# A fused attention and expert kernel: gates in a ring of five, one block sum formed later and in place, scratch shared

## The chip, the cores and the metric

The kernel runs on one core of one Trainium2 chip. Times are device microseconds of one execution. The engines are TensorE (PE, with PEld for its weight loads), VectorE (DVE), ScalarE (ACT), GpSimd (POOL) and the Sync engine (SP), from whose queue the stores of the output and the loads of the gates are issued.

A ratio of two kernels is the mean time of one kernel's runs over that of the other's of the same rounds, with a 95% interval, so it is not quite the ratio of the medians that stand beside it.

## The reference, cut to what matters

```python
def reference(**kwargs):            # cut: q, k, v are [4, 8, 768, 64]
    # attention: 4 sink keys, and a causal window of 128 keys
    attn_out = _attn_ref(**attn_kwargs)
    x = attn_out.transpose(0, 2, 1, 3).reshape(3072, 512)
    # four experts, every token through all of them
    p = domain_probs / (domain_probs.sum(-1, keepdims=True) + 1e-09)
    out = 0
    for e in range(4):
        h = np.maximum(x @ w1[e], 0.0)          # [3072, 1024]
        out += p[:, e:e + 1] * (h @ w2[e])      # [3072, 512]
    return out
```

## The kernel before

Tokens are handled in pairs of two 128-row tiles: three pairs a batch element, twelve pairs. The first batch element is done directly. For the other nine pairs, the second product (H times w2) is done with seven block products instead of eight (the scheme of Strassen and Winograd), P1 to P7. It needs sums of blocks of H on VectorE, in which H11 and H12 are the two halves of the first row tile and H21 and H22 those of the second. For each pair and each expert:

```python
# first product: 4 groups (j) of 8 matmuls per expert, each group evicted by VectorE
nc.vector.scalar_tensor_tensor(out=dst, in0=h, scalar=0.0, in1=gate, op0=ALU.max, op1=ALU.mult)
...
# sums(): as soon as an H block (all four groups of an expert) is there
nc.vector.tensor_add(S[0][:, e], H21, H22)          # operand of P5
nc.vector.tensor_sub(H21, H11, H21)                 # operand of P7, in place
nc.vector.tensor_sub(S[1][:, e], S[0][:, e], H11)   # operand of P6
...
for u in list(self.last):                           # operand of P3
    b, g, e = u
    if busy((b, g), "P3") or t["dve"] < self.stored:
        break
    ...
    nc.vector.tensor_sub(S[2][:, e], self.H[b, g, e][:, 1, :, 0], S[1][:, e])
...
CHAIN = ("P1", "P2", "P6", "P5", "P7", "P4", "P3")  # order of the products of a pair
```

The program is laid out by a scheduler inside the kernel's Python, which keeps its own estimate of each engine's time and picks the next piece of TensorE work. In a late pair it alternates products with single groups of H for the next pair (P1, group, P2, group, ..., P3), and then issues the ten remaining groups of that next pair without a product between. I call that the **dense stretch**. There are six H buffers. H groups go through four PSUM banks, which VectorE must empty.

The softmax here doesn't subtract the row's maximum and nothing guards it: scores larger than these inputs give would overflow.

Of the kernel before, what the change touches and what calls it, by code (L numbers as in the profile page):

```python
# [16 lines left out]
def kernel(  # L17
# [12 lines left out]
    nc = tc.nc  # L30
# [29 lines left out]
    TURN = 3500  # L60
# [6 lines left out]
    bank_free = {tag: [0.0] * n for tag, n in (("mix", 1), ("r", 4))}  # L67
# [24 lines left out]
    def free_at(tag, n=1):  # L92

        return max(bank_free[tag][:n])

    def take(tag, until):
        bank_free[tag].pop(0)
        bank_free[tag].append(until)
# [157 lines left out]
    dp = mo.tile([NT, P, E], FP32, name="dp", tag="osb", bufs=1)  # L256
# [4 lines left out]
    def gates_by_row():  # L261
        ds = mo.tile([NT, P], FP32, name="ds", tag="ds", bufs=1)
        pn = mo.tile([NT, E, P], FP32, name="pn", tag="hr", bufs=1)
        nc.vector.reduce_sum(out=ds, in_=dp, axis=AX.X)
        nc.vector.tensor_scalar_add(out=ds, in0=ds, scalar1=1e-9)
        nc.vector.reciprocal(out=ds, in_=ds)
        nc.vector.tensor_mul(
            pn, dp.rearrange("n p e -> n e p"), ds[:, None, :].to_broadcast([NT, E, P]),
        )
        for i in range(2):  # L270
            nc.sync.dma_start(out=gate_rows[:, :, i, :], in_=pn[i:NT:2])
        dve(1800, 0.0)
# [3 lines left out]
    def load_gates(pair):  # L276

        x = mo.tile([P, E, 2, P], FP32, name="gates", tag="gates", bufs=2)
        nc.sync.dma_start(
            out=x.rearrange("p e t n -> p (e t n)"),  # L280
            in_=gate_rows[pair].rearrange("e t n -> (e t n)").partition_broadcast(P),
        )
        gate_sb[pair] = x
        sp()
# [3 lines left out]
    zeros = mo.tile([P, 2 * G], BF16, name="zeros", tag="hr", bufs=1)  # L288
# [9 lines left out]
    identf = consts.tile([P, P], FP32, name="identf")  # L298
# [76 lines left out]
    def two_banks(tag="mix"):  # L375

        if tag == "mix":
            x = psum.tile([P, 2, 2 * G], FP32, name="sps", tag="mix", bufs=1)
            return [x[:, 0], x[:, 1]], x
        return [psum.tile([P, 2 * G], FP32, name="sps", tag=tag, bufs=4) for _ in range(2)], None  # L380

    def transposes(b, g, hp, tag="mix"):

        if b not in qkT:
            qkT[b] = sb.tile([P, 2, NHP, S], BF16, name="qkT", tag="qkT", bufs=1)
        if (b, g, hp) == (0, 0, 0):
            cast_first(0)
        tr = psum.tile([P, 2, 2, P], BF16, name="tr", tag=tag, bufs=1 if tag == "mix" else 4)
        hs = slice(2 * hp, 2 * hp + 2)
        for i in range(2):  # L390
            for tt in range(2):
                rows = first["qk"[i]][:, tt, hs] if (b, g) == (0, 0) else nat[b, 2 * g + tt][:, i, hs]
                nc.tensor.transpose(tr[:, i, tt], rows, ident)  # L393
        done = pe(4 * P, cast_at[hp // 2] if (b, g) == (0, 0) else rows_at(b, g), free_at(tag), n=4)
        dst = qkT[b][:, :, hp, g * G:(g + 1) * G]
        if (b, g) == (0, 0):
            for i, engine in enumerate(("dve", "act")):
                copy(engine, dst[:, i].rearrange("c (p t) -> c p t", t=2), tr[:, i].rearrange("c t p -> c p t"))
            at = max(act(2 * P, done), dve(2 * P, done))
        else:  # L400
            engine, at = sooner(4 * P, done)
            copy(engine, dst, tr.rearrange("c i t p -> c i (t p)"))
        take(tag, at)
        turned_at[b, g, hp] = at
        if (b, g, hp) == (0, 0, 1):
            cast_first(1)
        if hp == NHP - 1:
            for _ in range(2):
                qkn_free.remove(1e12)
                qkn_free.append(done)  # L410
            qkn_free.sort()
# [11 lines left out]
    def sink_values(b):  # L423
        vsd[b] = sb.tile([P, NHP, 2, DX], BF16, name="vsd", tag="vsd", bufs=2)
# [11 lines left out]
    def sinks(b, piece):  # L436
# [4 lines left out]
        sp, _ = two_banks()  # L441
# [14 lines left out]
    def scores(b, hp, g, tag="mix"):  # L456
        T = qkT[b]
        w = sum(x[2] for x in GROUPS[g]) * P
        sps, both = two_banks(tag)
# [11 lines left out]
        scored_at[b] = done = pe(w, scores_ready(b, hp, g, tag), n=6, switch=2)  # L471
        a = sb.tile([P, 2, w], BF16, name="aT", tag="aT", bufs=4)
        m = mask0 if g == 0 else mask1
        if both is not None:
# [3 lines left out]
            take(tag, at)  # L478
            at = dve(2 * w, at, rate=1.92)
        else:  # L480
            for ph in range(2):
# [3 lines left out]
                take(tag, at)  # L485
# [6 lines left out]
    def values(b, hp, g, tag="r"):  # L492

        ready = values_ready(b, hp, g, tag)
        od = psum.tile([P, 2, 2, DX], FP32, name="od", tag=tag, bufs=4)
# [34 lines left out]
        take(tag, at)  # L530
# [12 lines left out]
    def values_ready(b, hp, g, tag="r"):  # L543
        return max(
            aT_at[b, hp, g], free_at(tag), sinkA_at.get((b, g), 0.0), landed.get(("v", b, 2 * g + 1), 1e12),
        )

    def turn(b, hp, g, tag="r"):

        o = onats[b, g]  # L550
        tx = psum.tile([P, 2, P], BF16, name="tx", tag=tag, bufs=4)
        for qi in range(2):
            nc.tensor.transpose(tx[:, qi], o[:, qi, hp], ident)
        done = pe(2 * P, turn_ready(b, hp, g, tag), n=2)
# [4 lines left out]
        take(tag, at)  # L559
        xT_at[b, hp, g] = at  # L560

    def turn_ready(b, hp, g, tag="r"):
        return max(onat_at[b, hp, g], free_at(tag))
# [100 lines left out]
    class Mixture:  # L664
# [38 lines left out]
        def emit_first(self):  # L703
# [7 lines left out]
            if b > 0 and e == 0 and j == 0:  # L711
                pair = b * NG + g
                for x in (pair, pair + 1):
                    if x not in gate_sb and x < B * NG:
                        load_gates(x)
            if (b, e, j) == (0, E - 1, 0) and NG not in gate_sb:
                load_gates(NG)
                load_gates(NG + 1)
# [4 lines left out]
            h = psum.tile([P, 2, G], FP32, name="hps", tag="r", bufs=4)  # L723
# [11 lines left out]
            if b == 0:  # L735
# [5 lines left out]
                take("r", at)  # L741
            else:
                gate = gate_sb[b * NG + g][:, e].rearrange("p t n -> p (t n)")[:, None, :].to_broadcast([P, 2, G])
# [4 lines left out]
                take("r", at)  # L748
# [3 lines left out]
            if j == QF - 1:  # L752
                if b == 0:
                    self.second += [(g, s, e) for s in range(2)]
                else:
                    self.waiting.append((b, g, e))
                    self.sums()

        def sums(self):
# [3 lines left out]

            for u in list(self.waiting):
# [3 lines left out]
                if (b, g) not in self.S:  # L768
                    self.S[b, g] = [None] * 3
# [13 lines left out]
            for u in list(self.last):  # L783
                b, g, e = u
                if busy((b, g), "P3") or t["dve"] < self.stored:
                    break
                S = self.S[b, g]
                if S[2] is None:
                    S[2] = mo.tile([P, E, QF, P], BF16, name="S2", tag="wide2", bufs=1)
                nc.vector.tensor_sub(S[2][:, e], self.H[b, g, e][:, 1, :, 0], S[1][:, e])  # L790
                self.S4_at[b, g, e] = dve(QF * P, rate=1.92)
                self.last.remove(u)

        def operand(self, b, g, e, m):
            H = self.H[b, g, e]
            if m in ("P1", "P2", "P4", "P7"):
                return {"P1": H[:, 0, :, 0], "P2": H[:, 1, :, 0], "P4": H[:, 1, :, 1], "P7": H[:, 0, :, 1]}[m]
            return self.S[b, g]["P5 P6 P3".split().index(m)][:, e]
# [16 lines left out]
        def emit_product(self):  # L815
# [39 lines left out]
            if m == "P4":  # L855
# [11 lines left out]
        def emit_second(self):  # L867
            ready = self.second_ready()
            g, s, e = self.second.pop(0)
            if g not in out_sb:  # L870
                out_sb[g] = mo.tile([P, 2, Dout], FP32, name="osb0", tag=f"wide{g}", bufs=1)
# [164 lines left out]
```

## Time and profile before

| | |
|---|---|
| time | 392.64 us median of 3 runs (391.69 to 392.68); the profiled execution took 391.01 us, span 389.3 us |
| PE / DVE / ACT busy | 374.0 / 257.4 / 100.7 us |
| PE's waits for the H eviction | 4.2 us in 10 waits |

The page's busy time by engine (share of the span, then the number of instructions):

```profile
PE 374.0 (96%) x3583; PEld 298.9 (77%) x3596; DVE 257.4 (66%) x567; ACT 100.7 (26%) x172; POOL 72.9 (19%) x98
```

The view of PE's waits: who waited for whom, microseconds in total, number of waits, longest. This is the largest of its entries:

```profile
PE hps L727 <- DVE H L744: 4.2, 10, 0.9
```

The groups of instructions by line (out<-in, shapes, count, then busy us and mean ns of one, then the idle time before them): the H groups on PE, their eviction on VectorE, and the four block sums.

```profile
L727 PE MATMUL hps<-xT,w 128*128 128x256 bf16 x1536 | 186.9, 273 | 5.2 <-DVE H L744 4.2 <-DMA w<-in_moe_w_dram 0.8
L744 DVE SCALAR_TENSOR_TENSOR H<-hps,gates 128x512 bf16<-128x512 f32 x144 | 94.1, 684 | 25.1 <-PE hps L727 24.3
...
L776 DVE TENSOR_TENSOR H<-H 128x512 bf16<-128x512 bf16 x36 | 15.3, 425 | 1.2
L775 DVE TENSOR_TENSOR S<-H 128x512 bf16<-128x512 bf16 x36 | 15.3, 425 | 6.9 <-PE acc L825 5.7
L790 DVE TENSOR_TENSOR S<-H,S 128x512 bf16<-128x512 bf16 x36 | 15.2, 423 | 0.9
L777 DVE TENSOR_TENSOR S<-S,H 128x512 bf16<-128x512 bf16 x36 | 15.1, 418 | 0.0
```

The timeline of PE in a late dense stretch (start us, length us, group, count, and in brackets the idle time before it with its releaser). The ten groups are 80 matmuls:

```profile
309.27 1.91 PE L825 MATMUL acc<-w,S 128*128 128x256 bf16 x16
311.02 8.02 PE L727 MATMUL hps<-xT,w 128*128 128x256 bf16 x72
319.26 1.03 PE L727 MATMUL hps<-xT,w 128*128 128x256 bf16 x8 [0.22 <-DVE H L744]
320.13 1.91 PE L825 MATMUL acc<-w,H 128*128 128x256 bf16 x16
```

And VectorE in the same stretch:

```profile
314.42 2.48 DVE L744 SCALAR_TENSOR_TENSOR H<-hps,gates 128x512 bf16<-128x512 f32 x4
316.93 0.42 DVE L775 TENSOR_TENSOR S<-H 128x512 bf16<-128x512 bf16 x1
317.39 0.42 DVE L776 TENSOR_TENSOR H<-H 128x512 bf16<-128x512 bf16 x1
317.73 0.42 DVE L777 TENSOR_TENSOR S<-S,H 128x512 bf16<-128x512 bf16 x1
318.18 0.43 DVE L790 TENSOR_TENSOR S<-H,S 128x512 bf16<-128x512 bf16 x1
318.52 2.48 DVE L744 SCALAR_TENSOR_TENSOR H<-hps,gates 128x512 bf16<-128x512 f32 x4
```

One H block costs VectorE 318.52 - 314.42 = 4.10 us here, without a gap. TensorE's four groups of a block, 32 matmuls at 109 ns (16 products start 1.75 us apart: 311.02 - 309.27), take 3.5 us. So in the dense stretches VectorE sets the pace once the four banks are full. Outside of them, products without evictions give it time to catch up.

The late stretches are the clearest to read, but not the largest part of the loss. Three of the ten waits stand in them, 0.22 us each. The other seven, 3.5 us, stand between 134 and 266 us, where H groups follow each other between pieces of attention, and VectorE has masks and output scaling besides. The longest of all, on PE:

```profile
265.23 1.91 PE L727 MATMUL hps<-xT,w 128*128 128x256 bf16 x16 [0.92 <-DVE H L744]
```

and the eviction that it waits for, on VectorE, with the last block sum just before it:

```profile
264.15 0.42 DVE L790 TENSOR_TENSOR S<-H,S 128x512 bf16<-128x512 bf16 x1
264.50 0.68 DVE L744 SCALAR_TENSOR_TENSOR H<-hps,gates 128x512 bf16<-128x512 f32 x1
```

A matmul is shown with 273 ns, but in a stream the next one starts after 109 ns.

### The profile page before, as it was taken

To read this page: it belongs to the slowest core of one execution; us is meant where nothing else is said; L and a number is where in the kernel's file an instruction comes from. 1 tells how busy PE (TensorE), PEld (TensorE's weight loads), DVE (VectorE), ACT (ScalarE), POOL (GpSimd) and SP (SyncE) were. 2 spreads that over 40 slices of the span, in tenths; PEclk is the share of its full clock that TensorE was granted. 3 is DMA by queue.
4 is the path that set the end of the run, shared out by engine and by line. 5 is a ranking of instruction groups with operands and counts; after the bars stand their busy time and mean duration, and the time that the engine had idled before them with its cause. 6 is when DMAs were issued, how large, how long until landed. Compare 5 with 4: busy or idle time off the path is not lost.

```text
span 389.3 us, 8348 instructions
## 1 busy us (share of the span) xinstructions
PE 374.0 (96%) x3583; PEld 298.9 (77%) x3596; DVE 257.4 (66%) x567; ACT 100.7 (26%) x172; POOL 72.9 (19%) x98
## 2 busy tenths in 40 slices
PE   7889999999999999999999999999999999999995
PEld 3566767676667878878878878877888888888884
DVE  5573756653536997696698597678476495594660
ACT  4657433455443031321221231220100000000000
POOL 7964115400291138001200000000000000000000
PEclk9999999999999999999999999999999999999999
DMA  9999999934199999807492112013011011100101
GB/s 156 175 183 206 210 210 165 120 25 125 26 164 165 144 178 156 94 0 109 72 202 68 29 56 83 2 55 83 2 54 56 2 56 54 56 3 0 56 2 54
DMA packets 106913, 35.54 MB, mean 91 GB/s; under 512 B 93828, under 2 KB 101092, under 8 KB 106876
## 3 DMA queue, kind: packets, MB, share of 16 engines
q0 software_dynamic: 77520, 17.31, 50.7%
q1 hardware_dynamic: 29356, 17.70, 18.7%
q8 instruction: 28, 0.46, 0.5%
q14 instruction: 9, 0.07, 0.1%
HBM read 40.45 MB, written 6.34 MB: 120 GB/s over the span
## 4 chain that ended last, share of the span: by engine, by line
PE 73%; DVE 17%; DMA 3%; ACT 3%; POOL 2%; issue 1%; SPq 0%
PE acc L825 28%; PE hps L727 28%; PE acc L880 10%; DVE H L744 7%; PE sps L464 2%; PE od L514 2%; DMA w<-in_moe_w_dram 2%; DVE S L790 2%; DVE S L775 2%; DVE aT L476 2%; DMA qkT<-qkn 2%; DVE H L776 2%; DVE S L777 1%; ACT aT L475 1%; PE tr L393 1%
## 5 line engine op out<-in xcount | busy, mean ns | idle before, releaser
L727 PE MATMUL hps<-xT,w 128*128 128x256 bf16 x1536 | 186.9, 273 | 5.2 <-DVE H L744 4.2
L727 PEld LDWEIGHTS <-w 128*128 128x128 bf16 x1536 | 145.9, 98 | 29.8 <-issue 10.5
L744 DVE SCALAR_TENSOR_TENSOR H<-hps,gates 128x512 bf16<-128x512 f32 x144 | 94.1, 684 | 25.1 <-PE hps L727 24.3
L825 PEld LDWEIGHTS <-H 128*128 128x128 bf16 x576 | 56.0, 98 | 7.4 <-issue 0.9
L475 ACT ACTIVATE aT<-sps 128x1024 bf16<-128x1024 f32 (+1 forms) x42 | 40.2, 957 | 68.9 <-PE sps L464 65.5
L839 ACT COPY osb<-acc 128x256 f32<-128x256 f32 x36 | 13.4, 373 | 168.1 <-PE acc L825 168.1
L825 PEld LDWEIGHTS <-S 128*128 128x128 bf16 x432 | 41.8, 98 | 5.2 <-issue 0.5
L880 PE MATMUL acc<-w,H 128*128 128x512 bf16 x179 | 43.4, 379 | 0.8 <-issue 0.2
L476 DVE TENSOR_TENSOR aT<-aT,mask 128x1024 bf16<-128x1024 bf16 (+1 forms) x42 | 27.5, 655 | 20.4 <-ACT aT L475 19.0
L199 POOL DMA_DIRECT2D vx<-in_v_dram x24 | 21.4, 901 | 84.4 <-PE od L514 64.2
L738 ACT ACTIVATE H<-hps 128x512 bf16<-128x512 f32 x48 | 28.9, 603 | 26.9 <-PE hps L727 26.7
L825 PE MATMUL acc<-wf,H 128*128 128x256 bf16 x288 | 34.4, 273 | 0.5 <-ACT osb L839 0.5
L825 PE MATMUL acc<-w,S 128*128 128x256 bf16 x288 | 34.4, 273 | 0.0
L825 PE MATMUL acc<-w,H 128*128 128x256 bf16 x288 | 34.2, 273 | 0.0
L880 PEld LDWEIGHTS <-H 128*128 128x128 bf16 x192 | 18.3, 98 | 17.5
L890 DVE SCALAR_TENSOR_TENSOR osb<-acc,scale_t,osb 128x512 f32<-128x512 f32 x18 | 13.5, 751 | 21.0 <-PE acc L880 21.0
L133 POOL DMA_DIRECT2D qkn<-in_q_dram x22 | 19.9, 904 | 8.9 <-DMA w<-in_moe_w_dram 4.1
L133 POOL DMA_DIRECT2D qkn<-in_k_dram x22 | 19.9, 904 | 8.8 <-DMA w<-in_moe_w_dram 8.5
L526 DVE TENSOR_TENSOR onat<-od,R 128x256 bf16<-128x256 f32 x48 | 20.4, 424 | 1.7
L514 PE MATMUL od<-vx,aT 128*128 128x65 bf16 x352 | 20.3, 193 | 0.8 <-DVE aT L476 0.7
L514 PEld LDWEIGHTS <-aT 128*128 128x128 bf16 x352 | 17.2, 97 | 4.4 <-DVE aT L476 2.3
L775 DVE TENSOR_TENSOR S<-H 128x512 bf16<-128x512 bf16 x36 | 15.3, 425 | 6.9 <-PE acc L825 5.7
(72 smaller groups left out, 237.5 us busy)
## 6 DMA issues: line engine op xcount, KB each, us to landing
w<-in_moe_w_dram POOLq DMA_DIRECT2D x7, 1024.0 KB, 18.8
out_dram<-osb SPq DMA_DIRECT2D x24, 256.0 KB
gates<-gate_rows SPq DMA_DIRECT2D x9, 512.0 KB
vx<-in_v_dram POOLq DMA_DIRECT2D x24, 128.0 KB, 6.5
qkn<-in_q_dram POOLq DMA_DIRECT2D x22, 128.0 KB, 6.9
qkn<-in_k_dram POOLq DMA_DIRECT2D x22, 128.0 KB, 7.0
w<-in_moe_w_dram POOLq DMA_DIRECT2D x2, 512.0 KB, 8.2
qraw<-in_q_dram SPq DMA_DIRECT2D x2, 256.0 KB
```

The costliest lines, as they stand in the source:

```text
L133: nc.gpsimd.dma_start(out=both[:, i], in_=src[b, :, tb * P:(tb + 1) * P, :].rearrange("h p d -> p h d"),)
L199: nc.gpsimd.dma_start(out=vx[tb][:, :, 0:D], in_=v[b, :, tb * P:(tb + 1) * P, :].rearrange("h p d -> p h d"),)
L475: nc.scalar.activation(out=a, in_=both[:, :, 0:w], func=AF.Exp, scale=scale)
L476: nc.vector.tensor_mul(a, a, m[:, None, :].to_broadcast([P, 2, w]))
L514: nc.tensor.matmul(od[:, qi, ph], lhsT=a[:, ph, c:c + P], rhs=vx[kb][:, 2 * hp + ph, 0:DX], start=(g == 0 and i == 0), stop=(i == len(term ...
L526: nc.vector.tensor_mul(o[:, :, hp].rearrange("p q (h d) -> p q h d", h=2), od[:, :, :, 0:D], R.to_broadcast([P, 2, 2, D]),)
L727: nc.tensor.matmul(h[:, i].rearrange("p (q n) -> p q n", q=2), lhsT=w1_sb[e][:, db, fb * P:(fb + 1) * P], rhs=xT[b, g][:, :, db], start=(i ...
L738: nc.scalar.activation(out=dst, in_=h, func=AF.Relu)
L744: nc.vector.scalar_tensor_tensor(out=dst, in0=h, scalar=0.0, in1=gate, op0=ALU.max, op1=ALU.mult,)
L775: nc.vector.tensor_add(S[0][:, e], H21, H22)
L825: nc.tensor.matmul(x, lhsT=self.operand(b, g, e, m)[:, f], rhs=forms[e][m][:, f], start=(i == 0 and m in ("P1", "P2", "P5")), stop=(i == n ...
L880: nc.tensor.matmul(op, lhsT=H[:, fb // QF, fb % QF, s], rhs=w2_sb[e][:, fb, :], start=(fb == 0), stop=(fb == NFB - 1),)
```

## The change

Its intent is to save SBUF memory: gates are loaded per expert (128 KB) in a ring of five, where whole pairs (512 KB) were held in two buffers; the last block sum takes the place of H12, so that its tile S2 goes; early scratch shares the tiles of the derived weights. Its core:

```diff
-    def load_gates(pair):
-        x = mo.tile([P, E, 2, P], FP32, name="gates", tag="gates", bufs=2)
+    def load_gates():                       # next (pair, expert); called as each H block is done
+        x = mo.tile([P, 2, P], FP32, name="gates", tag="gates", bufs=NGATE)      # NGATE = 5
 ...
+            for u in list(self.last):       # in sums(), ahead of the other three sums
+                b, g, e = u
+                if (b, g, "P5") in self.products:
+                    break
+                H12 = self.H[b, g, e][:, 1, :, 0]
+                nc.vector.tensor_sub(H12, H12, S[1][:, e])
 ...
-            for u in list(self.last):       # after the other three sums
-                if busy((b, g), "P3") or t["dve"] < self.stored:
-                    break
-                nc.vector.tensor_sub(S[2][:, e], self.H[b, g, e][:, 1, :, 0], S[1][:, e])
 ...
-            if m == "P4":
+            if m == "P3":
                 self.live -= E              # H buffers counted as free
 ...
-            h = psum.tile([P, 2, G], FP32, name="hps", tag="r", bufs=4)
+            slot = pick()                   # of four banks, the one estimated to come free first
+            h = bank(slot, [P, 2, G], FP32, "hps")
 ...
-    dp = mo.tile([NT, P, E], FP32, name="dp", tag="osb", bufs=1)
+    scratch = wpool.tile([P, 12 * P], FP32, name="scratch", tag=f"wf_{E - 1}")
+    dp = scratch[0:NT, 0:4 * P].rearrange("n (p e) -> n p e", e=E)
```

(Cut: the other scratch tiles, one buffer fewer for the sink values, the same bank choice for the other users of the banks.) The last sum now cannot be issued when its H block is done: H12 is still read by P2. It is issued for all four experts at once after P5, the fourth product.

More of the change, by code (lines that the diff above doesn't have):

```diff
@@ L58 @@
     ]
-    TURN = 3500
+    NGATE = 5
     DX = D + 1
@@ L66 @@
     t = {"pe": 1200.0, "act": 0.0, "dve": 0.0, "pool": 3350.0, "sp": 800.0, "sw": 6100.0, "hw": 0.0}
-    bank_free = {tag: [0.0] * n for tag, n in (("mix", 1), ("r", 4))}
+    mix_free, ring = [0.0], [0.0] * 4
     WARM = 6600.0
@@ L92, in free_at, with pick, bank, take @@
     def free_at(tag, n=1):
-        return max(bank_free[tag][:n])
-    def take(tag, until):
-        bank_free[tag].pop(0)
-        bank_free[tag].append(until)
+        return mix_free[0] if tag == "mix" else sorted(ring)[n - 1]
+    def pick(among=range(4)):
+        return min(among, key=lambda i: ring[i])
+    def bank(i, shape, dtype, name):
+        return psum.tile(shape, dtype, name=name, tag=f"r{i}", bufs=1)
+    def take(i, until):
+        if i == "mix":
+            mix_free[0] = until
+        else:
+            ring[i] = until
     landed = {}
@@ L255 @@
     NT = Ntok // P
-    dp = mo.tile([NT, P, E], FP32, name="dp", tag="osb", bufs=1)
+    scratch = wpool.tile([P, 12 * P], FP32, name="scratch", tag=f"wf_{E - 1}")
+    dp = scratch[0:NT, 0:4 * P].rearrange("n (p e) -> n p e", e=E)
+    pn = scratch[0:NT, 4 * P:8 * P].rearrange("n (e p) -> n e p", e=E)
+    ds = scratch[0:NT, 8 * P:9 * P]
+    identf = scratch[:, 9 * P:10 * P]
     nc.sync.dma_start(out=dp, in_=moe_domain_probs.rearrange("(tb p) e -> tb p e", p=P))
@@ L261, in gates_by_row @@
     def gates_by_row():
-        ds = mo.tile([NT, P], FP32, name="ds", tag="ds", bufs=1)
-        pn = mo.tile([NT, E, P], FP32, name="pn", tag="hr", bufs=1)
         nc.vector.reduce_sum(out=ds, in_=dp, axis=AX.X)
@@ L274 @@
     gate_sb = {}
-    def load_gates(pair):
-        x = mo.tile([P, E, 2, P], FP32, name="gates", tag="gates", bufs=2)
+    def load_gates():
+        if len(gate_sb) == E * NG * (B - 1):
+            return
+        pair, e = divmod(len(gate_sb) + E * NG, E)
+        x = mo.tile([P, 2, P], FP32, name="gates", tag="gates", bufs=NGATE)
         nc.sync.dma_start(
-            out=x.rearrange("p e t n -> p (e t n)"),
-            in_=gate_rows[pair].rearrange("e t n -> (e t n)").partition_broadcast(P),
-        )
-        gate_sb[pair] = x
-        sp()
+            out=x.rearrange("p t n -> p (t n)"), in_=gate_rows[pair, e].rearrange("t n -> (t n)").partition_broadcast(P),
+        )
+        gate_sb[pair, e] = x
+        sp(takes=300)
     held = consts.tile([P, 2], BF16, name="held")
-    zeros = mo.tile([P, 2 * G], BF16, name="zeros", tag="hr", bufs=1)
+    zeros = wpool.tile([P, 2 * G], BF16, name="zeros", tag=f"wf_{E - 2}")
     nc.vector.memset(zeros, 0.0)
@@ L297 @@
         )
-    identf = consts.tile([P, P], FP32, name="identf")
     ident = consts.tile([P, P], BF16, name="ident")
@@ L378, in two_banks @@
             x = psum.tile([P, 2, 2 * G], FP32, name="sps", tag="mix", bufs=1)
-            return [x[:, 0], x[:, 1]], x
-        return [psum.tile([P, 2 * G], FP32, name="sps", tag=tag, bufs=4) for _ in range(2)], None
+            return [x[:, 0], x[:, 1]], x, ["mix"]
+        at = sorted(range(4), key=lambda i: ring[i])[:2]
+        return [bank(i, [P, 2 * G], FP32, "sps") for i in at], None, at
     def transposes(b, g, hp, tag="mix"):
@@ L387, in transposes @@
             cast_first(0)
-        tr = psum.tile([P, 2, 2, P], BF16, name="tr", tag=tag, bufs=1 if tag == "mix" else 4)
+        if tag == "mix":
+            i, tr = tag, psum.tile([P, 2, 2, P], BF16, name="tr", tag="mix", bufs=1)
+        else:
+            i = pick()
+            tr = bank(i, [P, 2, 2, P], BF16, "tr")
+        slot = i
         hs = slice(2 * hp, 2 * hp + 2)
@@ L402, in transposes @@
             copy(engine, dst, tr.rearrange("c i t p -> c i (t p)"))
-        take(tag, at)
+        take(slot, at)
         turned_at[b, g, hp] = at
@@ L423, in sink_values @@
     def sink_values(b):
-        vsd[b] = sb.tile([P, NHP, 2, DX], BF16, name="vsd", tag="vsd", bufs=2)
+        vsd[b] = sb.tile([P, NHP, 2, DX], BF16, name="vsd", tag="vsd", bufs=1)
         if b:
@@ L440, in sinks @@
         q0, q1 = piece * G, (piece + 1) * G
-        sp, _ = two_banks()
+        sp, _, _ = two_banks()
         for hp in range(NHP):
@@ L458, in scores @@
         w = sum(x[2] for x in GROUPS[g]) * P
-        sps, both = two_banks(tag)
+        done = scores_ready(b, hp, g, tag)
+        sps, both, slots = two_banks(tag)
         c = 0
@@ L470, in scores @@
             c += nq * P
-        scored_at[b] = done = pe(w, scores_ready(b, hp, g, tag), n=6, switch=2)
+        scored_at[b] = done = pe(w, done, n=6, switch=2)
         a = sb.tile([P, 2, w], BF16, name="aT", tag="aT", bufs=4)
@@ L477, in scores @@
             at = act(2 * w, done)
-            take(tag, at)
+            take("mix", at)
             at = dve(2 * w, at, rate=1.92)
@@ L484, in scores @@
                 at = act(w, done)
-                take(tag, at)
+                take(slots[ph], at)
                 at = dve(w, at, rate=1.92)
@@ L490, in scores_ready, with values @@
         return max(free_at(tag, 1 if tag == "mix" else 2), *turned(b, g, hp))
-    def values(b, hp, g, tag="r"):
-        ready = values_ready(b, hp, g, tag)
-        od = psum.tile([P, 2, 2, DX], FP32, name="od", tag=tag, bufs=4)
+    def values(b, hp, g):
+        ready = values_ready(b, hp, g)
+        slot = pick()
+        od = bank(slot, [P, 2, 2, DX], FP32, "od")
         a = aTs.pop((b, hp, g))
@@ L529, in values @@
         at = dve(2 * P, done)
-        take(tag, at)
+        take(slot, at)
         onat_at[b, hp, g] = at
@@ L541, in values, with values_ready, turn @@
         values_at[b, g] = done
-    def values_ready(b, hp, g, tag="r"):
+    def values_ready(b, hp, g):
         return max(
-            aT_at[b, hp, g], free_at(tag), sinkA_at.get((b, g), 0.0), landed.get(("v", b, 2 * g + 1), 1e12),
+            aT_at[b, hp, g], free_at("r"), sinkA_at.get((b, g), 0.0), landed.get(("v", b, 2 * g + 1), 1e12),
         )
-    def turn(b, hp, g, tag="r"):
+    def turn(b, hp, g):
         o = onats[b, g]
-        tx = psum.tile([P, 2, P], BF16, name="tx", tag=tag, bufs=4)
+        ready = turn_ready(b, hp, g)
+        slot = pick()
+        tx = bank(slot, [P, 2, P], BF16, "tx")
         for qi in range(2):
             nc.tensor.transpose(tx[:, qi], o[:, qi, hp], ident)
-        done = pe(2 * P, turn_ready(b, hp, g, tag), n=2)
+        done = pe(2 * P, ready, n=2)
         if (b, g) not in xT:
@@ L558, in turn, with turn_ready @@
         copy(engine, xT[b, g][:, :, hp], tx)
-        take(tag, at)
+        take(slot, at)
         xT_at[b, hp, g] = at
-    def turn_ready(b, hp, g, tag="r"):
-        return max(onat_at[b, hp, g], free_at(tag))
+    def turn_ready(b, hp, g):
+        return max(onat_at[b, hp, g], free_at("r"))
     class Attention:
@@ L710, in emit_first @@
             self.first.pop(0)
-            if b > 0 and e == 0 and j == 0:
-                pair = b * NG + g
-                for x in (pair, pair + 1):
-                    if x not in gate_sb and x < B * NG:
-                        load_gates(x)
-            if (b, e, j) == (0, E - 1, 0) and NG not in gate_sb:
-                load_gates(NG)
-                load_gates(NG + 1)
+            if (b, e, j) == (0, E - 1, 0) and not gate_sb:
+                for _ in range(NGATE):
+                    load_gates()
             if j == 0:
@@ L722, in emit_first @@
                 self.live += 1
-            h = psum.tile([P, 2, G], FP32, name="hps", tag="r", bufs=4)
+            slot = pick()
+            h = bank(slot, [P, 2, G], FP32, "hps")
             for i in range(2):
@@ L740, in emit_first @@
                     nc.vector.tensor_scalar(out=dst, in0=h, scalar1=0.0, scalar2=None, op0=ALU.max)
-                take("r", at)
+                take(slot, at)
             else:
-                gate = gate_sb[b * NG + g][:, e].rearrange("p t n -> p (t n)")[:, None, :].to_broadcast([P, 2, G])
+                gate = gate_sb[b * NG + g, e].rearrange("p t n -> p (t n)")[:, None, :].to_broadcast([P, 2, G])
                 nc.vector.scalar_tensor_tensor(
@@ L747, in emit_first @@
                 at = dve(2 * G, end, fixed=152)
-                take("r", at)
+                take(slot, at)
             self.H_at[b, g, e] = max(at, self.H_at[b, g, e])
@@ L755, in emit_first @@
                 else:
+                    load_gates()
                     self.waiting.append((b, g, e))
@@ L762, in busy @@
                 return any(x[2] == m and x[:2] != pair for x in self.products[:len(CHAIN)] if x[:2] < pair)
+            for u in list(self.last):
+                b, g, e = u
+                if (b, g, "P5") in self.products:
+                    break
+                S = self.S[b, g]
+                H12 = self.H[b, g, e][:, 1, :, 0]
+                nc.vector.tensor_sub(H12, H12, S[1][:, e])
+                self.S4_at[b, g, e] = dve(QF * P, rate=1.92)
+                self.last.remove(u)
             for u in list(self.waiting):
@@ L768, in sums @@
                 if (b, g) not in self.S:
-                    self.S[b, g] = [None] * 3
+                    self.S[b, g] = [None] * 2
                     for i in range(2):
@@ L782, in sums @@
                 self.last.append(u)
-            for u in list(self.last):
-                b, g, e = u
-                if busy((b, g), "P3") or t["dve"] < self.stored:
-                    break
-                S = self.S[b, g]
-                if S[2] is None:
-                    S[2] = mo.tile([P, E, QF, P], BF16, name="S2", tag="wide2", bufs=1)
-                nc.vector.tensor_sub(S[2][:, e], self.H[b, g, e][:, 1, :, 0], S[1][:, e])
-                self.S4_at[b, g, e] = dve(QF * P, rate=1.92)
-                self.last.remove(u)
         def operand(self, b, g, e, m):
             H = self.H[b, g, e]
-            if m in ("P1", "P2", "P4", "P7"):
-                return {"P1": H[:, 0, :, 0], "P2": H[:, 1, :, 0], "P4": H[:, 1, :, 1], "P7": H[:, 0, :, 1]}[m]
-            return self.S[b, g]["P5 P6 P3".split().index(m)][:, e]
+            if m in ("P5", "P6"):
+                return self.S[b, g]["P5 P6".split().index(m)][:, e]
+            return {"P1": H[:, 0, :, 0], "P2": H[:, 1, :, 0], "P3": H[:, 1, :, 0], "P4": H[:, 1, :, 1], "P7": H[:, 0, :, 1]}[m]
         def product_ready(self):
@@ L870, in emit_second @@
             if g not in out_sb:
-                out_sb[g] = mo.tile([P, 2, Dout], FP32, name="osb0", tag=f"wide{g}", bufs=1)
+                out_sb[g] = mo.tile([P, 2, Dout], FP32, name="osb0", tag=f"wide{g}" if g < 2 else "osb", bufs=1)
                 if g == 0:
```

## The prediction

> **What bounds the kernel.** TensorE. The page's busy table gives PE 374.0 us of 389.3 (96%), at full granted clock. Sixteen 128x256 products take 1.75 us, and the change leaves their number as it is: the instruction order has the same 7187 PE rows and the same 32 filler products. So only PE's idle 15 us can be won. The waits of PE name VectorE's H eviction for 4.2 us, all after 130 us. By windows over the stages from 126 to 372 us, PE misses 4.9 us, nearly all in the stretches where H blocks follow each other without products between. There VectorE is full (9.79 of 10 us at 130-140, 9.83 at 200-210, 9.72 at 260-270): the timeline shows 4 evictions (0.61 us apart) and 4 block sums (0.42 us each) per H block, 4.1 us, against 3.5 us of PE.
>
> **What the change does.**
> 1. The last block sum (36 x 423 ns = 15.2 us of VectorE) is not removed. It leaves the dense stretches and is issued as four back-to-back operations (1.7 us) after the fourth product, P5, in place of H12. There VectorE is idle about half of the time in the late stages. Each dense stretch loses about 3 to 4 sums, 1.3 to 1.7 us, more than PE's wait in it (0.2 to 1.5 us).
>    In place should cost the same: the H21 sum is already in place (425 ns against 423); the Trainium skill, "VectorE: DVE Perf Modes", "Mode 2×_1P", asks for 16-bit data with step 1, which both have.
> 2. P3 now waits for these sums. After P5 come P7, P4 and two H groups (5.2 us of PE), or 3.5 us for the last pair, against 1.7 us of sums: no wait. H slots come free at P3 rather than P4; the order of PE work shows no harm from it.
> 3. Gates: 36 loads of 128 KB for 9 of 512 KB, same bytes. A load is issued when the block five before it was evicted, 14 us of PE work or more ahead. 27 more issues of 0.33 us don't fill the Sync queue. Neutral.
> 4. Shared scratch, smaller vsd, bank choice by earliest predicted release: memory is saved that nothing here uses; the order is unchanged up to 126 us. Neutral.
>
> **On the critical path:** of 4.9 us missed at 126-372, about 0.5 is a wait for a key transpose (137 us), which stays. Of the rest I expect 2.5 to 4 us back; new small VectorE collisions in the attention stages (masks and output scaling behind a 1.7 us block of sums) return some 0.5 us. Net about -2.8 us.
>
> **Predicted time: 389.8 us** (8 in 10: 387.8 to 392.4). Chances: faster by over 2% 0.02, within 2% 0.96, slower by over 2% 0.02.
>
> **Right if the profile shows:** PE waiting for the H eviction under 1.5 us in total (4.2 before); a late pair lasting 26.3 us instead of 26.6; no PE wait of products on the in-place sum; first 126 us within 0.3 us; the sum still about 425 ns x36; H evictions without a wait for gates.
>
> **What would make it wrong:** gate loads landing late behind transposes in the Sync queue (evictions waiting for a DMA); VectorE's block of four sums delaying evictions or masks so that the four PSUM banks run full during P7 and P4; P3 waiting for its sums; bank choices by a wrong model making PE wait for a bank in the mixed stages.

## The result

The changed kernel takes 386.82 us (median of 4 runs, 385.04 to 387.3) against 392.66 us: ratio 0.9843, interval 0.9804 to 0.9883. The gain is 5.8 us where 2.8 was forecast, and the time lies under the forecast range. The two profiled executions differ by less, 391.01 to 387.30 us; where the difference lies is shown below. The interval stands for 4.6 to 7.7 us; two repeats gave 5.4 and 4.1 us by the medians, so some of the 5.8 us is likely chance, and about 5 us is what has to be explained.

The same lines after, the view of PE's waits, then the groups by line:

```profile
PE hps L745 <- DVE H L762: 0.6, 2, 0.5
```

```profile
L762 DVE SCALAR_TENSOR_TENSOR H<-hps,gates 128x512 bf16<-128x512 f32 x144 | 94.7, 684 | 27.3 <-PE hps L745 27.1
...
L789 DVE TENSOR_TENSOR H<-H,S 128x512 bf16<-128x512 bf16 x36 | 12.8, 417 | 0.0
```

The last sum is still there 36 times and takes as long as before for one (417 ns; its total is smaller only because four in a row overlap). PE's waits for evictions are down to 0.6 us in 2 waits. None of VectorE's waits names a gate load. The dense stretch after, on PE:

```profile
305.61 1.91 PE L843 MATMUL acc<-w,H 128*128 128x256 bf16 x16
307.36 8.90 PE L745 MATMUL hps<-xT,w 128*128 128x256 bf16 x80
316.09 1.91 PE L843 MATMUL acc<-w,H 128*128 128x256 bf16 x16
```

And on VectorE: a block in the dense stretch now takes 314.82 - 311.17 = 3.65 us, against 3.5 us of PE; the four moved sums stand later, where it had time.

```profile
311.17 2.48 DVE L762 SCALAR_TENSOR_TENSOR H<-hps,gates 128x512 bf16<-128x512 f32 x4
313.68 0.43 DVE L803 TENSOR_TENSOR S<-H 128x512 bf16<-128x512 bf16 x1
314.14 0.43 DVE L804 TENSOR_TENSOR H<-H 128x512 bf16<-128x512 bf16 x1
314.48 0.42 DVE L805 TENSOR_TENSOR S<-S,H 128x512 bf16<-128x512 bf16 x1
314.82 2.48 DVE L762 SCALAR_TENSOR_TENSOR H<-hps,gates 128x512 bf16<-128x512 f32 x4
...
324.15 0.69 DVE L762 SCALAR_TENSOR_TENSOR H<-hps,gates 128x512 bf16<-128x512 f32 x1 [1.93 <-PE hps L745]
324.76 1.42 DVE L789 TENSOR_TENSOR H<-H,S 128x512 bf16<-128x512 bf16 x4
326.77 0.69 DVE L762 SCALAR_TENSOR_TENSOR H<-hps,gates 128x512 bf16<-128x512 f32 x1 [0.59 <-PE hps L745]
```

**A wait in PE's timeline is under-read.** The 80 matmuls of the dense stretch took 320.13 - 311.02 = 9.11 us before and 316.09 - 307.36 = 8.73 us after: 0.38 us saved. But the only wait shown before is 0.22 us. The missing 0.16 us is the difference between the shown length of a matmul and the distance to the next one, 273 - 109 ns = 0.164 us: for so long after the last matmul's real successor was due, PE is still shown as busy. (By the same reckoning a delay shorter than that would not show at all.) The Trainium skill says where this comes from: "Perfetto Trace Analysis", section "Tensor Engine Instruction (MATMUL, LD_WEIGHTS)", has the end of a matmul estimated by the profiler, not observed; "TensorE: Matmul & The Clock Gate" gives (398 + N) / 2.4 ns for a single matmul ("Single matmul latency") and N / 2.4 + 2.5 ns between two ("Back-to-back issue gap"), which for N = 256 are 272.5 and 109.2 ns. This trace agrees with both (273 and 109), although that section keeps the second formula for an isolated pair, and here it fits streams in which every matmul has its own weight load.

The same on the whole late part. The order of PE's work is the same in both kernels up to the start of the first long dense stretch, so I count from the start of the sink product just before it (125.18 us before, 126.41 us after) to the end of the span. The windows view gives length, then the busy times of PE, PEld, DVE, ACT and POOL with counts, the granted clock, the DMA share and GB/s; first before, then after:

```profile
125.18:389.30 264.12, 254.57 (x2506) 219.34 (x2503) 186.95 (x399) 37.44 (x64) 18.57 (x22) 1.00 0.40 63
```

```profile
126.41:385.60 259.19, 253.53 (x2506) 219.25 (x2503) 185.25 (x399) 37.37 (x64) 18.56 (x22) 1.00 0.44 66
```

The late part is 4.93 us shorter. PE's idle time falls by 3.89 us (9.55 to 5.66), and its "busy" time by another 1.04 us with the same 2506 matmuls: that part was waiting, shown as work. By the waits view: 4.2 - 0.6 = 3.6 us shown, and 8 waits fewer at 0.164 us, 1.3 us: 4.9 us.

**The first 125 us differ between executions.** They took 1.23 us longer in the changed kernel's profile, with the same order of PE's work. Among the 14 profiles this point is reached between 125.2 and 127.7 us. Two things differ there from one execution to the next: PE's waits for the first weight loads, and, in some executions, the granted clock. Here are the windows of two executions with the same early order, the third profile of the changed kernel and that of a variant (`tail`, below):

```profile
20.00:30.00 10.00, 9.40 (x100) 6.35 (x99) 6.60 (x20) 6.17 (x11) 6.09 (x8) 0.85 1.82 182
```

```profile
20.00:30.00 10.00, 8.85 (x103) 6.11 (x102) 6.52 (x21) 5.93 (x12) 6.07 (x8) 1.00 1.83 181
```

The clock was granted at 0.85 in that window in one and in full in the other. Over 19.52 to 22.93 us of after_third the windows view gives 0.50. A stretch like it, 3.4 us long, stands in the first 32 us of three of the 14 profiles (after_again, after_third, moved_only), the three that reach the point last, at 126.9 to 127.7 us. "TensorE: Matmul & The Clock Gate", section "What's actually happening", has the clock depend on how busy the array has been recently, but both of these executions have a wait of PE for weights of 2.0 us ahead of the window, so that wait alone does not decide it, and the cause stays open.

That all of the early difference is chance is not shown. The waits for weight loads come to 1.2 to 2.4 us in the seven profiles with the new gates and scratch, and to 0.3 to 1.4 us in the seven with the old; the point is reached at 126.7 and 125.9 us in the mean. No run takes gates and scratch apart. The timed ratio of after_sums_early, below, speaks against a loss that lasts: its interval leaves at most 0.2 us. So this stays open. For the comparisons below, the late part, counted from the same point, is therefore the sharper measure, beside the timed ratios.

### The profile page after: what moved, and what is told of

Read it like the earlier page. It is cut to its first block, busy times and chain, and to the rows that moved or that the text cites. A ratio compares the mean times of both kernels' runs of the same rounds, so it can differ in the third digit from the quotient of the medians. Undisturbed runs are those within 1.5% of the kernel's fastest.

```text
span 385.6 us, 8412 instructions
## 1 busy us (share of the span) xinstructions
PE 372.6 (97%) x3583; PEld 298.4 (77%) x3596; DVE 255.4 (66%) x567; ACT 101.0 (26%) x172; POOL 72.9 (19%) x98
## 4 chain that ended last, share of the span: by engine, by line
PE 76%; DMA 15%; DVE 4%; POOL 3%; issue 1%; ACT 0%; SPq 0%
PE hps L745 34%; PE acc L843 29%; DMA w<-in_moe_w_dram 7%; PE acc L898 6%; DMA qkn<-in_k_dram 6%; PE sps L483 3%; PE od L534 2%; DMA qkT<-qkn 2%; DVE H L762 2%; POOL vx L208 1%; POOL qkn L142 1%; PE tr L411 1%; PE od L527 1%; POOL w L220 0%; PE sps L461 0%
## 5 line engine op out<-in xcount | busy, mean ns | idle before, releaser
L843 PEld LDWEIGHTS <-H 128*128 128x128 bf16 x720 | 70.0, 98 | 9.1 <-issue 0.9
L843 PE MATMUL acc<-w,H 128*128 128x256 bf16 x432 | 51.4, 273 | 0.0
L495 DVE TENSOR_TENSOR aT<-aT,mask 128x1024 bf16<-128x1024 bf16 (+1 forms) x42 | 27.3, 651 | 28.0 <-ACT aT L494 26.2
L898 PEld LDWEIGHTS <-H 128*128 128x128 bf16 x192 | 18.4, 98 | 17.7
L843 PEld LDWEIGHTS <-S 128*128 128x128 bf16 x288 | 28.0, 98 | 3.4 <-issue 0.2
L483 PE MATMUL sps<-qkT 64*128 64x128 bf16 (+1 forms) x256 | 17.7, 240 | 1.3 <-ACT qkT L178 0.6
L861 DVE TENSOR_TENSOR osb<-osb,acc 128x256 f32<-128x256 f32 x18 | 7.6, 421 | 16.3 <-PE acc L843 14.1
```

The costliest lines, as they stand in the source:

```text
L483: nc.tensor.matmul(sps[ph][:, c:c + nq * P], lhsT=T[pr, 1, hp, kb * P:(kb + 1) * P], rhs=T[pr, 0, hp, qb * P:(qb + nq) * P], start=True, s ...
L495: nc.vector.tensor_mul(a, a, m[:, None, :].to_broadcast([P, 2, w]))
L843: nc.tensor.matmul(x, lhsT=self.operand(b, g, e, m)[:, f], rhs=forms[e][m][:, f], start=(i == 0 and m in ("P1", "P2", "P5")), stop=(i == n ...
L898: nc.tensor.matmul(op, lhsT=H[:, fb // QF, fb % QF, s], rhs=w2_sb[e][:, fb, :], start=(fb == 0), stop=(fb == NFB - 1),)
```

## The experiments

Theory 1: the whole gain is VectorE's relief in the dense stretches, because the last sum runs later. Theory 2: the parts that I had called neutral (gates, banks, scratch) give what was not forecast. A third possibility, the new order of PE's work that the scheduler makes of the change, is tested too.

Summary; "late part" is from the point named above to the span's end, of the profiled execution; the last column is what the waits view gives: change of the waits for H evictions, plus 0.164 us for each change in their number.

| kernel | median us (before) | ratio, interval | late part us | against before | by waits |
|---|---|---|---|---|---|
| before | | | 264.1 | | |
| changed | 386.82 (392.66) | 0.9843, 0.9804-0.9883 | 259.2 | -4.9 | -4.9 |
| after_again | 386.78 (392.14) | 0.9864, 0.9843-0.9886 | 258.8 | -5.3 | -4.9 |
| sums_only | 387.29 (392.14) | 0.9880, 0.9856-0.9904 | 259.2 | -4.9 | -4.9 |
| moved_only | 387.08 (392.14) | 0.9867, 0.9839-0.9894 | 259.2 | -4.9 | -4.9 |
| after_sums_early | 391.78 (392.14) | 0.9986, 0.9967-1.0006 | 264.0 | -0.1 | +0.4 |
| no_last_sum | 387.31 (392.08) | 0.9870, 0.9846-0.9894 | 258.8 | -5.3 | -4.9 |
| old_order_no_sum | 387.77 (392.08) | 0.9894, 0.9867-0.9921 | 259.6 | -4.6 | -4.9 |
| half_moved | 390.03 (392.08) | 0.9949, 0.9916-0.9981 | 260.9 | -3.2 | -3.3 |
| one_more_sum | 402.23 (392.08) | 1.0257, 1.0234-1.0280 | 274.4 | +10.3 | +10.0 |
| after_third | 387.38 (391.51) | 0.9882, 0.9855-0.9909 | 259.1 | -5.0 | -4.9 |
| nh7 | 387.04 (391.51) | 0.9866, 0.9825-0.9907 | 258.7 | -5.4 | -4.9 |
| tail | 385.68 (391.51) | 0.9851, 0.9818-0.9884 | 257.3 | -6.8 | not of H waits alone |
| tail_again | 385.83 (391.87) | 0.9832, 0.9797-0.9867 | 257.7 | -6.4 | not of H waits alone |

### after_again: the changed kernel once more

> The changed kernel once more, for a tighter ratio and a second profile. If the measured 5.8 us is real, the ratio lies at 0.984 to 0.986 (about 5.5 to 6 us less than before). If part of it was chance of which executions were drawn (before's profiled execution took 391.0 us, 1.6 us less than its median), the ratio is nearer 0.988 to 0.990, the 3.7 us that the two profiled executions differ by. Theory of the early noise: the first 126 us differ between two profiles of the same kernel by up to about 1 us, with PE waits for weight loads.

Measured: 386.78 us, 5.4 us less than before, ratio 0.9864: just outside the first expectation, and better than the second. The 5 us are real; the 3.7 us between the first two profiles are the 4.9 us of the late part less the 1.2 us by which the early parts differed. This profile reached the point above 1.3 us later than the first profile of the same kernel.

### sums_only: only the last sum changed

The kernel before, with the sum's place, its time and the count of H buffers as in the change (the diff is cut to its core):

```diff
+                if (b, g, "P5") in self.products:
+                    break
+                nc.vector.tensor_sub(H12, H12, S[1][:, e])
-                nc.vector.tensor_sub(S[2][:, e], self.H[b, g, e][:, 1, :, 0], S[1][:, e])
-            if m == "P4":
+            if m == "P3":
```

> The kernel before with only the last block sum changed: formed in place of H12 after P5, H slots free at P3. Theory 1 (the relief of VectorE in the dense stretches is all of the gain): 5 to 6 us less than before, PE wait for the H eviction under 1 us. Theory 2 (the other parts, gates, banks, scratch, give the part that I had not predicted): only 2 to 3.5 us less.

Measured: 4.8 us less than before by the medians, 4.9 us in the late part, waits for the eviction 0.6 us. The order of PE's instructions is exactly that of the changed kernel. This is just under the 5 to 6 us of theory 1, and well over the 2 to 3.5 us of theory 2: theory 1 stands.

### moved_only: the sum moved in time, not in place

```diff
-                if busy((b, g), "P3") or t["dve"] < self.stored:
+                if (b, g, "P5") in self.products or busy((b, g), "P3") or t["dve"] < self.stored:
```

(With this loop put ahead of the other three sums, since the next pair's sums overwrite S1.)

> The kernel before with the last block sum only moved in time: after P5, but still into its own tile S2, H slots free at P4 as before. If it is the time of issue that counts and not the place: the same as sums_only within 0.7 us. If the in-place form or the later release of H matters: different by over 1 us.

Measured: 5.1 us less than before. It is the time of issue alone: with its own tile, and H buffers counted as free at P4, the gain is the same within the 0.7 us set. The in-place form saves memory; a gain in time from it is not seen. PE's order is that of the changed kernel here too.

### after_sums_early: everything but the sum

The changed kernel with the diff of sums_only undone.

> The changed kernel with the last block sum put back as before (own tile, issued as soon as the H block is there), gates, banks and scratch as changed. Theory 1: equal to before within 0.8 us, PE wait for the H eviction back at about 4 us. Theory 2: 2 to 3.5 us faster than before.

Measured: 0.4 us less than before, an interval that includes no change, and a late part of 264.0 us; the waits for the H eviction are back at 4.4 us. PE's order is exactly that of before, so the bank choice changed no order. Gates, banks and scratch together give nothing that 5 rounds can see. Theory 2 falls.

### no_last_sum: the moved sum taken away

Wrong result; against sums_only:

```diff
-                nc.vector.tensor_sub(H12, H12, S[1][:, e])
                 self.S4_at[b, g, e] = dve(QF * P, rate=1.92)
```

> Wrong result on purpose: sums_only with the last block sum taken away altogether (P3 multiplies the plain H12), TensorE order as in sums_only and in the changed kernel. If the moved sums cost nothing where they now stand (no collisions, against the 0.5 us that I had predicted): equal to sums_only (387.3 us) within 0.7 us. If they collide with masks, evictions and products: 0.5 to 1.5 us less than sums_only.

Measured: 387.31 us, where sums_only took 387.29 on another chip; late parts 258.8 and 259.2 us. Where they now stand, 15 us of VectorE work have no cost that these runs can see: the 0.4 us between the late parts is as much as the changed kernel's own profiles differ by.

### old_order_no_sum: the sum taken away in the old order

Wrong result: the kernel before, its scheduler still counting the sum, but the instruction left out and P3 reading H12.

```diff
-                nc.vector.tensor_sub(S[2][:, e], self.H[b, g, e][:, 1, :, 0], S[1][:, e])
                 self.S4_at[b, g, e] = dve(QF * P, rate=1.92)
```

> Wrong result on purpose: the kernel before without the last block sum (P3 multiplies the plain H12), with exactly the TensorE order of before. If VectorE's load in the dense stretches was the cause: the same 4.8 to 5.5 us as the moved sums give. If the new order of TensorE's work gave part of the gain: only 3 to 4 us. PE waits for the H eviction under 1 us in either case.

Measured: 4.3 us less by the medians, 4.6 us in the late part: between the two expectations. The waits for the H eviction fall to 0.6 us with PE's order unchanged, those between 134 and 266 us as well as those in the late stretches. VectorE's load explains nearly all. The new order may add up to 0.8 us (late part 259.6 us, against 258.8 of no_last_sum, which has the new order); the intervals overlap, so this small part stays open.

### one_more_sum: the dose doubled

The kernel before, the last sum done twice into the same tile, order of PE unchanged:

```diff
                 nc.vector.tensor_sub(S[2][:, e], self.H[b, g, e][:, 1, :, 0], S[1][:, e])
+                nc.vector.tensor_sub(S[2][:, e], self.H[b, g, e][:, 1, :, 0], S[1][:, e])
```

> The kernel before with the last block sum done twice into the same tile, order of TensorE unchanged, right result: 36 x 423 ns = 15.2 us more of VectorE, about three sums of it in each of the nine dense stretches. If VectorE sets the pace there, each microsecond added in them is one of time: 8 to 13 us slower. If the banks' slack takes up much of it: under 5 us. Theory of the under-read waits: time added = PE waits added for the H eviction + about 0.16 us for each wait added.

Measured: 10.1 us slower for 15.2 us of VectorE work. The waits view and a dense stretch:

```profile
PE hps L727 <- DVE H L744: 12.9, 18, 1.6
```

```profile
319.14 4.53 PE L727 MATMUL hps<-xT,w 128*128 128x256 bf16 x40
323.98 3.65 PE L727 MATMUL hps<-xT,w 128*128 128x256 bf16 x32 [0.32 <-DVE H L744]
328.55 1.03 PE L727 MATMUL hps<-xT,w 128*128 128x256 bf16 x8 [0.91 <-DVE H L744]
329.42 1.91 PE L826 MATMUL acc<-w,H 128*128 128x256 bf16 x16
```

The 80 matmuls now take 329.42 - 319.14 = 10.28 us, 1.17 us more than before, close to three sums of 0.42 us. Two waits of 0.32 and 0.91 us with twice 0.164 us make 1.56 us over the unhindered 8.73 us, which is just that. The rule for reading waits holds here too: 8.7 us more waiting and 8 waits more predict 10.0 us, and the late part grew by 10.3.

### half_moved: half the dose

The kernel before, the last sum moved after P5 for experts 2 and 3 only (the same condition, preceded by `e >= E // 2 and`, in a loop before and after the other sums).

> The kernel before with the last sum moved after P5 for experts 2 and 3 only, into the tile S2 as before. If the loss is VectorE's demand over TensorE's time in each dense stretch, two of the three sums in it taken out leave little: 3 to 4.7 us less than before, more than half of the full 5. If the gain is in proportion: 2.5 us less.

Measured: the late part of the profiled run is 3.2 us shorter, two thirds of the full gain. In the late dense stretches the trace shows only one of the three last sums gone, not two as expected, since those of experts 0 and 1 still run there (309.45 and 311.96 us); yet PE's wait is gone and the 80 matmuls take 8.73 us (308.91 to 317.64), as with all of them moved. There one third of the dose gives all of the gain, as a demand does that only counts where it exceeds PE's time. For the whole kernel this is less clear, since PE's order is here neither that of before (it differs between 141 and 223 us) nor that of the changed kernel. The timed ratio shows less (2.0 us, an interval from 0.7 to 3.3, which holds both expectations): four of its six runs had a mean granted clock of 0.991 to 0.996, of the 11 runs of before two. The two at 0.999 and above took 388.2 us, 3.7 us under the nine runs of before with 0.998 or more (mean 391.9), but that choice was made after the fact. So the threshold shape is supported by the profile and not by the timing.

### after_third and nh7: does the freed memory help?

after_third is the changed kernel; nh7 differs in one line:

```diff
-    NH = 6
+    NH = 7
```

> The changed kernel a third time, to stand beside the next two on the same chip: 386 to 387.5 us, 5 to 5.8 us less than before.

> The changed kernel with seven H blocks instead of six, in the memory that the change frees. TensorE's waits after 126 us are only 1.1 to 1.6 us in all: no gain, within 0.6 us of the changed kernel. If the H slots, held until P3, were a limit: 0.6 us or more faster.

Measured: after_third 387.38 us, 4.1 us less than before by the medians (4.6 by the ratio), under the 5 to 5.8 expected; its late part is 5.0 us shorter. nh7 387.04 us with overlapping intervals. PE's order is the same, instruction by instruction. The memory saved gains no time here.

### tail: a version that beats both

With PE's waits gone, the changed kernel's end is what one can see in the timeline (SPq is the Sync engine's queue):

```profile
377.85 1.91 PE L843 MATMUL acc<-wf,H 128*128 128x256 bf16 x16 [0.46 <-ACT osb L857]
...
379.59 1.91 PE L843 MATMUL acc<-w,H 128*128 128x256 bf16 x16
379.79 0.37 ACT L857 COPY osb<-acc 128x256 f32<-128x256 f32 x1 [2.00 <-PE acc L843]
381.54 0.42 DVE L861 TENSOR_TENSOR osb<-osb,acc 128x256 f32<-128x256 f32 x1 [3.29 <-PE acc L843]
381.99 0.33 SPq L870 DMA_DIRECT2D out_dram<-osb  x1
382.41 0.38 SPq L877 DMA_DIRECT2D out_dram<-osb  x1
```

(The rows of weight loads are left out.) P4 waits for the eviction of P7 from the same bank, and both stores of the last pair go out at the very end, though the second one's data were ready at 380.2 us. For the last pair only:

```diff
-            self.products = [(b, g, m) for b, g in PAIRS for m in CHAIN]
+            self.products = [(b, g, m) for b, g in PAIRS for m in (CHAIN if (b, g) != PAIRS[-1] else CHAIN[:5] + ("P3", "P4"))]
 ...
+            if m == "P5" and final:         # P5 leaves its bank by itself, before P7
+                nc.scalar.copy(out=C22, in_=x)
+            if final and m == "P7":
+                nc.vector.tensor_add(C22, C22, x)
 ...
+            if final and m in ("P2", "P7", "P3", "P4"):       # each quarter of the output as it is done
+                i, c = {"P2": (0, 0), "P7": (1, 1), "P3": (0, 1), "P4": (1, 0)}[m]
+                nc.sync.dma_start(out=out[r + i * P:r + (i + 1) * P, c * G:(c + 1) * G], in_=o[:, i, c * G:(c + 1) * G])
```

> The changed kernel with another ending of its last pair: P5 evicted by itself, P3 before P4, and four stores of half rows, each as soon as its quarter of the output is there. The trace shows at the end one PE wait of 0.46 us on an eviction (0.6 us with the 0.16 us that such a reading hides), and two stores of 256 KB issued at 381.99 and 382.41 us, though one was ready at 380.2. Expected: 1.0 to 1.6 us less than the changed kernel of the same call, 385 to 386 us. If the end is set by the latency of the last store alone and not by its size and place: only 0.6 us less.

> The other ending once more, since its first ratio's interval (0.9818 to 0.9884) overlaps that of the changed kernel of the same call (0.9855 to 0.9909). If its gain of about 1.5 us over the changed kernel is real: ratio to before 0.982 to 0.985, and 257 to 257.5 us from the start of the first long H stretch to the end, against 258.8 to 259.2 us of the changed kernel's three profiles. If it was chance: ratio 0.986 to 0.988.

Measured: 385.68 and 385.83 us, ratios 0.9851 and 0.9832; late parts 257.3 and 257.7 us against 258.8 to 259.2 of the changed kernel's three profiles. The result is right. The first interval overlaps that of the changed kernel, so the timing alone does not prove it; the late parts support it, by about 1.5 us in two profiles against three, and the trace shows PE's wait gone and the earlier quarters' stores under way before the last eviction:

```profile
378.78 1.91 PE L844 MATMUL acc<-wf,H 128*128 128x256 bf16 x16
378.99 0.42 DVE L868 TENSOR_TENSOR osb<-osb,acc 128x256 f32<-128x256 f32 x1 [1.25 <-PE acc L844]
379.43 2.03 SPq L878 DMA_DIRECT2D out_dram<-osb  x2
380.73 0.37 ACT L864 COPY osb<-acc 128x256 f32<-128x256 f32 x1 [4.87 <-PE acc L844]
```

From the start of the last eviction to the end of the span it is 3.4 us here (384.1 - 380.73) against 4.1 us (385.6 - 381.54).

## Why the prediction was right or wrong

The mechanism was right and its size was not: 2.8 us forecast, 5.8 us in the first timing, about 5 us in the late parts and the repeats. The remaining 0.9 us has no cause in the traces and lies within the interval.

- **Right: VectorE sets the pace in the dense stretches, and moving the last sum frees it.** PE's waits for the eviction went from 4.2 to 0.6 us (forecast: under 1.5). sums_only and moved_only show that this is the gain, old_order_no_sum that it comes without a new order of PE's work, and one_more_sum that more of the same costs time.
- **Wrong, the term that failed: "of 4.9 us missed at 126-372 ... Of the rest I expect 2.5 to 4 us back".** The loss was read from idle time and waits as shown, 4.2 us for the evictions. Each of the ten waits hides 0.164 us, so the loss was 4.2 + 1.6 = 5.8 us, of which 0.6 + 0.3 = 0.9 us stays: 4.9 us back. Of PE's idle time as shown, 3.9 us came back, which is within the 2.5 to 4; the step that failed was to take the idle time shown for the whole loss. The trace of before held what was needed: 273 ns against 109 ns, and a late pair of 26.57 us (293.56 to 320.13) where 240 matmuls at 109.2 ns need 26.2.
- **Not borne out: "new small VectorE collisions ... return some 0.5 us".** no_last_sum finds no such cost in the timing; the 0.4 us between its late part and that of sums_only is within the noise of one profile, so a cost of that size is not excluded either.
- **Right: a late pair at 26.3 us instead of 26.6.** It takes 26.20 us (289.89 to 316.09). This line of the prediction did not fit its own sum: it gave back 0.3 us a pair where only 0.22 us was shown as waiting. The difference was the hint that waits hide something.
- **Right: in place costs the same.** 417 ns against 423. The skill's "VectorE: DVE Perf Modes", section "Mode 2×_1P", asks for 16-bit data with step 1, which both forms have; the trace has the same time for both, but no run shows which mode was taken.
- **Right: P3 does not wait for its sums, gates arrive in time, gates and banks and scratch are neutral in the timed runs** (after_sums_early, ratio 0.9986; the early profiles leave a doubt, see above). The order of PE's work changed with the sum; its own part, at most 0.8 us, is not settled.
- **Wrong: "first 126 us within 0.3 us".** They differed by 1.23 us. They differ by 1.3 us between profiles of the changed kernel alone, and by up to 2.5 us among all with the same early order of PE's work.

## What to carry to other kernels

When an engine beside the bottleneck is full in one stage and idle in another, work that is needed late is worth moving even if none of it is saved: here 15 us of sums moved and 5 us were gained. To size such a loss, compare the elapsed time of a stretch with the number of matmuls times their distance in an unhindered stretch, not with the idle time shown, since every wait of TensorE here hid 0.164 us, the part of a matmul's shown length that the next one overlaps in a stream. And compare from a point up to which the two orders agree, so that differences of the start stay out.

## What the Trainium skill lacked or had wrong

- "Perfetto Trace Analysis" says that a matmul's end is estimated, and "TensorE: Matmul & The Clock Gate" gives its latency and the distance of two; neither says what follows for reading waits: after a stall, PE is shown busy for their difference. Here 0.164 us per wait at 128x256, 1.3 of the 4.9 us saved in the late part; with it, waits gave the change of the late part within about 0.5 us in the seven variants with other sums. But four of the seven have the same waits as the changed kernel and one nearly those of before; the real tests are one_more_sum, +10.3 us (by waits +10.0), and half_moved, -3.2 us (-3.3).
- "TensorE: Matmul & The Clock Gate", section "What's actually happening", gives half and full rate and says that the first change to full rate comes at another time from run to run; it does not say that a half-rate stretch can come back in some executions of a kernel and not in others. Here 3 of 14 profiles have one of 3.4 us between 19.5 and 31.3 us, and mean granted clocks of single runs lie between 0.989 and 1.000, with one core running.
- The same page, "Back-to-back issue gap", says that its formula counts too much for wide matmuls in streams of weight load and matmul, and gives about 131 ns for N = 512 there. Here such a stream keeps to the formula: from the start of eight 128x512 matmuls to that of the next work it is 1.73 us (113.95 to 115.68 us in the kernel before), 216 ns each.
- Otherwise the pages agreed with the trace where they were used: 272.5 and 109.2 ns for a 128x256 matmul against 273 and 109 measured.
